# Batch 1's second scores a unit sooner, with k's evacuation on ScalarE, V copies on GpSimd, and W1 in 512-column pieces

## The chip, the cores and the metric

The kernel runs on one core of a Trainium2 chip. The metric is the device time in microseconds of one execution, as the median of several runs. A core has five engines that run side by side and meet at semaphores: TensorE (matrix products, and transposes by an identity), VectorE, ScalarE, GpSimd, and SyncE, which here only issues DMAs. Each engine takes its instructions in the order in which the program emits them, so an instruction that waits holds up all that follows it on its engine.

## The reference

```
# B, H, S, D = 8, 8, 576, 64
scores = q @ k^T / sqrt(D)                      # per batch and head
keep only 0 <= row - column < 64, softmax over columns
attn = softmax @ v                              # (B, H, S, D)
x  = attn with heads side by side               # (B, S, 512)
xn = (x - mean) / sqrt(var + 1e-6) * g_ln
out = x + relu(xn @ w_ch1) @ w_ch2              # 512 -> 2048 -> 512
```

Inputs and output are float32; the kernel computes its products in float16 with float32 sums.

## The kernel before, in words

The rows are cut into nine groups: group g (0 to 7) is the first 512 rows of batch g, group 8 the last 64 rows of all batches. A group has four blocks of 128 rows. Per block the attention is: **scores** (`s_pe`, L314, 32 small matmuls into PSUM), **exponentials** (`s_exp`, L350, ScalarE, two instructions), **mask** (`s_mask`, L362, VectorE, multiplies the probabilities by a 0/1 mask), **value step** (`b_pe`, L375, TensorE), and **rows** (`b_rows`, L397, VectorE: division by the row sums, mean and variance, and for groups 0 and 1 the z of the layer norm). `zt_step` (L461) transposes z; in groups 0 and 1 it does so on TensorE, with an evacuation from PSUM. The value step needs V in two layouts, `vA` (the block's rows) and `vB` (shifted by 64 rows): `vB_cur` and `vB_prev` (L181, L184) make the shifted one by copies across partitions. `t_main` (L259) transposes q (x=0) or k (x=1) of one half of a batch: eight transposes into PSUM and one evacuation by `evac` (L253), to ScalarE (0) or VectorE (1), x itself unless told otherwise.

The MLP of group g runs while the attention of batch g+1 is computed in between. `mlp_units` returns a list of units of TensorE work; after unit i, the steps that were put into slot i by `at(i, ...)` are emitted. So the order is written out by hand. Groups 0 and 1 start with half units (`l1_half`, L631: two 128-column chunks of W1 for 256 rows, eight matmuls of 256 columns). In group 0, two of them are replaced by `l1_rows` (L644), which works on one block of 128 rows at a time. The unit list of group 0 has 30 entries: eight of these, `l1` (L494) for the rest of W1, ten of `l2_three` (L672: the second layer for three blocks at once), and four parts of `l2` (L506) for the last block; `add_out` (L516, VectorE) then adds the product to x and frees its PSUM bank. Group 1 has 16 half units first. Their PSUM banks come from a pool of two (`ps_mm`), shared with the output banks of the second layer; each is free again when ScalarE has evacuated it with the relu (L641), or when `add_out` has read it.

W1 is loaded in eight pieces of 512 KB (`w1_load`, L195) on SyncE's queue, and scaled by g_ln into float16 by GpSimd or ScalarE (`w1_cast`, L213). The first four pieces hold all four 128-row chunks for 256 columns, the other four hold two chunks for 512 columns. W2 follows in eight pieces on the same queue (`w2_load`, `w2_cast`), with batch 1's q, k and V among them (`queue_up`, L940). `keep_clock(n)` (L882) emits n filler matmuls. `after_mask` (L359) is a one-column copy on GpSimd that reads the last masked probabilities, so that GpSimd's later instructions start after that mask. `part_vB` makes vB of later batches by DMA from vA.

Of the kernel before, what the change touches and what calls it, by code (L numbers as in the profile page):

```python
# [10 lines left out]
FP32 = mybir.dt.float32  # L11
# [7 lines left out]
def kernel(  # L19
# [166 lines left out]

    def part_vB(b, c, w=2):
        vB[b] = vB[b - 2]
        nc.sync.dma_start(out=vB[b][64:128, c:c + w], in_=vA[b][0:64, c:c + w])
        c0 = max(c, 1)  # L190
        nc.sync.dma_start(out=vB[b][0:64, c0:c + w], in_=vA[b][64:128, c0 - 1:c + w - 1])
# [3 lines left out]
    def w1_load(i):  # L195
        q2, pr = divmod(i, 2)
        if i < 4:
            t = p_wst.tile([128, NKC, HID // 8], FP32, tag="wld", name=f"w1s_{i}")[:, :, :]
            wst[("w1", i)] = t
            nc.sync.dma_start(  # L200
                out=t, in_=moe_w_ch1[:, (HID // 8) * i:(HID // 8) * (i + 1)].rearrange("(c p) n -> p c n", p=128),
            )
            return
        t = w2s[:, 4 * (i - 4):4 * (i - 3), :].rearrange("p c n -> p (c n)").bitcast(FP32).rearrange(
            "p (c n) -> p c n", c=2)
# [7 lines left out]
    def w1_cast(i, k0=0, k1=NKC, act=False):  # L213
        q2, pr = divmod(i, 2)
        t = wst[("w1", i)]
        if i < 4:
            for kc in range(k0, k1):
                o, sc = w1g[:, kc, (HID // 8) * i:(HID // 8) * (i + 1)], gT[:, kc:kc + 1]
                if act:
                    nc.scalar.activation(out=o, in_=t[:, kc], func=AF.Identity, bias=0.0, scale=sc)  # L220
                else:
                    nc.gpsimd.tensor_scalar(out=o, in0=t[:, kc], scalar1=sc, scalar2=1.0, op0=ALU.mult, op1=ALU.mult)
            return
        dst = w1g[:, 2 * pr:2 * pr + 2, (HID // 4) * q2:(HID // 4) * (q2 + 1)]
        for c in range(2):
            kc = 2 * pr + c
            nc.gpsimd.tensor_scalar(out=dst[:, c], in0=t[:, c], scalar1=gT[:, kc:kc + 1], scalar2=1.0,
                                    op0=ALU.mult, op1=ALU.mult)
# [256 lines left out]
    def mlp_units(g, split=0, three=False, seven=True):  # L485
# [158 lines left out]
        def l1_rows(kb):  # L644
            for i in range(2):
                if kb == 2:
                    pool, tag = ((ps_mm, "mm"), (ps_s, "sc"))[i]
                    rows_ps[i] = pool.tile([128, 2, 256], FP32, tag=tag, name=f"hph_{g}_1_{i}")
                c0 = 128 * (kb - 2)
                for e in range(2):  # L650
                    hc = 2 * i + e
                    for kc in range(NKC):
                        nc.tensor.matmul(
                            out=rows_ps[i][:, e, c0:c0 + 128], lhsT=w1g[:, kc, 128 * hc:128 * (hc + 1)],
                            rhs=zT[g][:, kc, 128 * kb:128 * kb + 128], start=(kc == 0), stop=(kc == NKC - 1),
                        )
                if kb == 3:
                    nc.scalar.activation(out=hrT[:, 2 * i:2 * i + 2, 256:512], in_=rows_ps[i],
                                         func=AF.Relu, bias=0.0, scale=1.0)

        rows_ps = {}

# [131 lines left out]
        if g == 0:  # L794
            halves = [(0, 0), (0, 1), (0, 2), 2, 3, (0, 3), (1, 2), (1, 3)]
        for u in halves:
            if isinstance(u, int):
                units.append(lambda u=u: l1_rows(u))
            else:
                units.append(lambda half=u[0], i=u[1]: l1_half(half, i))  # L800
# [120 lines left out]
    w1_cast(0, 0, 2)  # L921
    w1_cast(1, 0, 3)
    for i in range(2, 8):
        w1_cast(i)
# [10 lines left out]
    w1_cast(0, 2, 4, True)  # L935
    s_mm(0, 3, True)
    w1_cast(1, 3, 4, True)
    z_step(0, 2)

    def queue_up():  # L940
# [16 lines left out]
        cast_v(1, 2, 3)  # L957
        cast_v(1, 3, 4)
        load_qk(2, 0)
# [9 lines left out]
    for g in range(NGRP):  # L969
# [19 lines left out]
        if g == 0:  # L989
            at(0, b_step, 0, 3)  # L990
            at(0, queue_up)
            at(1, zt_step, 0, 2)
# [229 lines left out]
```

## Time and profile before

| | us |
|---|---|
| median of 3 runs | 304.95 (304.7 to 305.51) |
| the profiled execution's own time | 304.41 |
| its span, first to last instruction | 302.7 |
| TensorE busy | 292.3 (97%) |
| VectorE, ScalarE, GpSimd busy | 207.7, 156.2, 158.5 |
| mean granted TensorE clock | 0.996 |

The profile is one execution. In its timeline a row has the start, the busy time, the engine, the program line, the operation with the tiles written and read, the count, and in brackets the idle time of the engine ahead of it with what ended it. The span is shorter than the execution's time by 1.71 us, which lies around it.

### The profile page before, as it was taken

Reading aid. Unit: us, or ns where it says so; the run is one execution under the profiler, and the core shown is the slowest. Engines: PE = TensorE matmul, PEld = TensorE weight load, DVE = VectorE, ACT = ScalarE, POOL = GpSimd, SP = SyncE. Lnnn points to the kernel's source line nnn. Section 1 sums busy time; section 2 is a strip of 40 time slices with the busy share of each in tenths; the row PEclk is TensorE's granted clock in tenths of the full one; section 3 lists DMA queues with packets and bytes.
Section 4 is the critical chain, followed back from the end, with each engine's and each line's share of the span. In section 5 each row is a group of like instructions: output and inputs, shape, how many; then the busy total and the mean of one; then the engine's idle time right before and its main releaser. Section 6 shows DMA issues by size and latency. Waiting matters only on the chain.

```text
span 302.7 us, 7604 instructions
## 1 busy us (share of the span) xinstructions
PE 292.3 (97%) x3081; PEld 195.4 (65%) x3081; DVE 207.7 (69%) x408; ACT 156.2 (52%) x265; POOL 158.5 (52%) x238
## 2 busy tenths in 40 slices
PE   8999999989999999999999999999999999999992
PEld 3557545777454478547854786469646854788881
DVE  1881328684847886579766866698567775879972
ACT  3585645768358633874177428851664056216400
POOL 4689974543641886188608860897048307115200
PEclk9999999999999999999999999999999999999998
DMA  8999999999787999999299997992729396013014
GB/s 187 259 358 341 384 284 289 255 313 246 146 207 227 209 216 144 284 266 165 49 285 281 202 160 231 318 165 38 220 63 164 69 223 152 11 41 117 1 37 104
DMA packets 115044, 58.34 MB, mean 193 GB/s; under 512 B 83649, under 2 KB 106753, under 8 KB 115010
## 3 DMA queue, kind: packets, MB, share of 16 engines
q1 hardware_dynamic: 114720, 57.47, 79.7%
q8 instruction: 24, 0.39, 0.6%
q10 hardware_dynamic: 290, 0.40, 0.5%
q14 instruction: 10, 0.08, 0.1%
HBM read 38.80 MB, written 9.44 MB: 159 GB/s over the span
## 4 chain that ended last, share of the span: by engine, by line
PE 81%; DMA 7%; SPq 4%; ACT 3%; POOL 1%; issue 0%; DVE 0%
PE hps L494 28%; PE pA L571 12%; PE pB L571 8%; PE pC L571 8%; PE ch L506 5%; PE hph L636 5%; PE xps L394 3%; PE sc L347 3%; DMA w1s<-in_moe_w_ch_dram 3%; DMA wT<-in_moe_w_ch_dram 3%; PE lA L710 2%; DMA w2s<-in_moe_w_ch_dram 2%; SPq L167 2%; PE tp L274 2%; SPq L87 1%; PE lC L710 1%
## 5 line engine op out<-in xcount | busy, mean ns | idle before, releaser
L494 PE MATMUL hps<-zT,w1g 128*128 128x512 f16 x416 | 94.8, 379 | 0.0
L498 ACT ACTIVATE hrT<-hps 128x512 f16<-128x512 f32 x104 | 62.4, 600 | 41.2 <-PE hps L494 37.8
L494 PEld LDWEIGHTS <-w1g 128*128 128x128 f16 x416 | 39.2, 98 | 45.5 <-issue 2.2
L357 ACT ACTIVATE pt<-sc 128x512 f16<-128x512 f32 x72 | 39.5, 602 | 19.6 <-PE sc L347 18.8
L571 PEld LDWEIGHTS <-sS 128*128 128x128 f16 x448 | 43.3, 98 | 4.9
L446 POOL TENSOR_SCALAR rsz<-mvg 128x1 f32<-128x1 f32 x28 | 9.7, 346 | 69.3 <-DVE mvg L419 67.3
L367 DVE TENSOR_TENSOR pt<-pt,mask 128x1024 f16<-128x1024 f16 x32 | 23.4, 735 | 22.4 <-ACT pt L357 22.4
L145 POOL CAST qk<-qk 128x1024 f16<-128x1024 f32 x30 | 33.4, 1129 | 9.4 <-DMA qk<-in_q_dram 3.5
L571 PEld LDWEIGHTS <-hrT 128*128 128x128 f16 x336 | 32.1, 98 | 6.4 <-ACT hrT L498 1.0
L255 ACT COPY qkT<-tp 128x1024 f16<-128x1024 f16 (+1 forms) x17 | 16.4, 963 | 24.9 <-PE tp L274 22.9
L571 PE MATMUL pC<-w2s,sS 128*128 128x256 f16 x224 | 26.9, 273 | 0.0
L571 PE MATMUL pA<-wT,sS 128*128 128x256 f16 x224 | 26.9, 273 | 0.0
L414 DVE TENSOR_TENSOR xn<-xps,rcp 128x256 f32<-128x256 f32 (+1 forms) x50 | 25.8, 539 | 0.8
L416 DVE BATCH_NORM_STATS2 stats<-xn 128x6 f32<-128x512 f32 x36 | 25.0, 695 | 1.2
L545 DVE TENSOR_TENSOR sS<-hrT 128x512 f16<-128x512 f16 (+1 forms) x40 | 24.2, 605 | 2.1 <-ACT hrT L498 2.0
L636 PE MATMUL hph<-zT,w1g 128*128 128x256 f16 x176 | 22.3, 273 | 1.3 <-ACT hrT L641 0.4
L452 POOL TENSOR_SCALAR z<-xn,rsz 128x512 f16<-128x512 f32 x24 | 21.5, 895 | 2.5
L410 DVE RECIPROCAL rcp<-xps 128x4 f32<-128x4 f32 (+1 forms) x50 | 8.0, 181 | 19.0 <-PE xps L394 18.9
L447 POOL TENSOR_TENSOR rsz<-rsz,mhalf 128x1 f32<-128x1 f32 x28 | 18.5, 661 | 2.3
L636 PEld LDWEIGHTS <-w1g 128*128 128x128 f16 x176 | 16.4, 98 | 4.6 <-issue 1.3
L506 PE MATMUL ch<-w2s,hrT 128*128 128x512 f16 x80 | 18.8, 379 | 0.0
L173 POOL CAST vA<-v 128x1024 f16<-128x1024 f32 (+1 forms) x18 | 15.4, 873 | 4.9 <-DMA v<-in_v_dram 4.6
(121 smaller groups left out, 429.3 us busy)
## 6 DMA issues: line engine op xcount, KB each, us to landing
out_dram<-xn SPq DMA_DIRECT2D x33, 256.0 KB, 3.0
qk<-in_q_dram SPq DMA_DIRECT2D x16, 512.0 KB, 6.2
qk<-in_k_dram SPq DMA_DIRECT2D x16, 512.0 KB, 7.0
v<-in_v_dram SPq DMA_DIRECT2D x28, 256.0 KB, 6.9
w2s<-in_moe_w_ch_dram SPq DMA_DIRECT2D x9, 512.0 KB, 8.1
w1s<-in_moe_w_ch_dram SPq DMA_DIRECT2D x4, 512.0 KB, 7.4
tk<-in_k_dram SPq DMA_DIRECT2D x8, 256.0 KB, 4.7
tv<-in_v_dram SPq DMA_DIRECT2D x8, 256.0 KB, 5.2
```

Of the source, the lines that this page charges most:

```text
L145: nc.gpsimd.tensor_copy(out=dst[:, :].rearrange("p (a j) e d -> p a e j d", j=j), in_=t[:, :].rearrange("p (a e j d) -> p a e j d", e=2, j ...
L357: nc.scalar.activation(out=o, in_=i, func=AF.Exp, bias=0.0, scale=scale)
L367: nc.vector.tensor_tensor(out=ptv, in0=ptv, in1=mb, op=ALU.mult)
L414: nc.vector.tensor_tensor(out=xn[:, n * i:n * i + n], in0=xps[:, :, 0:D], in1=rcp_b, op=ALU.mult)
L416: nc.vector.bn_stats(out=stats, in_=xv)
L452: nc.gpsimd.tensor_scalar(out=z, in0=xv, scalar1=rs, scalar2=nm, op0=ALU.mult, op1=ALU.add)
L494: nc.tensor.matmul(out=hps, lhsT=w1g[:, kc, 128 * hc:128 * (hc + 1)], rhs=zT[g][:, kc, :], start=(kc == 0), stop=(kc == NKC - 1),)
L498: nc.scalar.activation(out=hrT[:, hc, :], in_=hps, func=AF.Relu, bias=0.0, scale=1.0)
L506: nc.tensor.matmul(out=ch[kb], lhsT=hrT[:, hc, 128 * kb:128 * (kb + 1)], rhs=w2s[:, hc, :], start=(hc == 0), stop=(hc == NHC - 1),)
L545: nc.vector.tensor_tensor(out=o, in0=x, in1=y, op=op)
L571: nc.tensor.matmul(out=o, lhsT=a[:, c, 128 * p:128 * p + 128], rhs=wv[:, c, :], start=(first and (p == 0 or split_c) and c == 0), stop=(c ...
L636: nc.tensor.matmul(out=hps[:, e], lhsT=w1g[:, kc, 128 * hc:128 * (hc + 1)], rhs=zT[g][:, kc, 256 * half:256 * half + 256], start=(kc == 0) ...
```

## The change

W1's first four pieces take the form of the other four: two 128-row chunks by 512 columns. `w1_cast` gets a list of chunks; GpSimd casts all but two chunks, the second ones of pieces 1 and 3, which ScalarE casts. Group 0's units become eight plain half units; `l1_rows` goes. Batch 0's last value step (`b_step(0, 3)`) moves from behind the first unit to ahead of it, behind two filler matmuls. The evacuation of z's block 2 moves from ScalarE to VectorE.

For batch 1's second half: k's evacuation moves from VectorE to ScalarE; the three shifted V copies move from ScalarE, in slots 27 and 28, to GpSimd, in `queue_up`; the scores of blocks 2 and 3 move from slot 29 to 28, ahead of group 0's last unit; block 3's exponentials come with them, and its mask moves from group 1 into slot 29. In group 1, the value steps move from slot 3 to 1, the z transposes from 6 and 7 to 4 and 6, and batch 2's transposes from 4, 5, 6, 7 to 2, 3, 5, 7. On GpSimd `after_mask` comes after one cast of batch 2 instead of three, and V's casts move from slot 5 to 0.

```diff
+    def shift_v(p, c):
+        nc.gpsimd.tensor_copy(out=vB[1][p:p + 64, c + (p == 0), :, 0:D], in_=vq(1, c, c + 1)[64 - p:128 - p, 0])
...
     def w1_load(i):
         q2, pr = divmod(i, 2)
         if i < 4:
-            t = p_wst.tile([128, NKC, HID // 8], FP32, tag="wld", name=f"w1s_{i}")[:, :, :]
...
+            t = p_wst.tile([128, 2, HID // 4], FP32, tag="wld", name=f"w1s_{i}")[:, :]
+        else:
...
-    def w1_cast(i, k0=0, k1=NKC, act=False):
+    def w1_cast(i, cs=(0, 1), act=False):
...
+        for c in cs:
             kc = 2 * pr + c
+            o, sc = w1g[:, kc, (HID // 4) * q2:(HID // 4) * (q2 + 1)], gT[:, kc:kc + 1]
+            if act:
+                nc.scalar.activation(out=o, in_=t[:, c], func=AF.Identity, bias=0.0, scale=sc)
+            else:
+                nc.gpsimd.tensor_scalar(out=o, in0=t[:, c], scalar1=sc, scalar2=1.0, op0=ALU.mult, op1=ALU.mult)
...
-        if g == 0:
-            halves = [(0, 0), (0, 1), (0, 2), 2, 3, (0, 3), (1, 2), (1, 3)]
...
-    w1_cast(0, 0, 2)
-    w1_cast(1, 0, 3)
-    for i in range(2, 8):
-        w1_cast(i)
+    for i in range(8):
+        w1_cast(i, (0,) if i in (1, 3) else (0, 1))
...
-    w1_cast(0, 2, 4, True)
     s_mm(0, 3, True)
-    w1_cast(1, 3, 4, True)
+    w1_cast(1, (1,), True)
     z_step(0, 2)
+    keep_clock(2)
+    b_step(0, 3)
...
         cast_qk(1, 1)
         cast_v(1, 2, 3)
+        shift_v(64, 2)
+        shift_v(0, 2)
         cast_v(1, 3, 4)
+        shift_v(64, 3)
...
         if g == 0:
-            at(0, b_step, 0, 3)
+            at(0, w1_cast, 3, (1,), True)
             at(0, queue_up)
-            at(1, zt_step, 0, 2)
+            at(1, zt_step, 0, 2, "dve")
...
-            at(26, t_main, 1, 1, 1, 1)
+            at(26, t_main, 1, 1, 1, 0)
             at(26, lambda: tbank.update(n=0))
             at(27, zt_step, 1, 1)
-            at(27, vB_cur, 1, 2, 0)
-            at(28, vB_prev, 1, 2, 0)
-            at(28, vB_cur, 1, 3, 0)
-            at(29, s_pe, 1, 2)
-            at(29, s_pe, 1, 3, False, "t")
-            at(29, s_exp, 1, 2, 0, 1)
-            at(29, s_mask, 1, 2)
+            at(28, s_pe, 1, 2)
+            at(28, s_pe, 1, 3, False, "t")
+            at(28, s_exp, 1, 2, 0, 1)
+            at(28, s_mask, 1, 2)
+            at(28, s_exp, 1, 3, 0, 1)
+            at(29, s_mask, 1, 3)
         if g == 1:
-            at(0, s_exp, 1, 3, 0, 1)
-            at(0, s_mask, 1, 3)
-            at(0, cast_qk, 2, 0)
-            at(0, cast_qk, 2, 1, (0,))
+            at(0, cast_qk, 2, 0, (0,))
             at(0, after_mask, 1, 3)
-            at(0, cast_qk, 2, 1, (1,))
-            at(3, b_pe, 1, 2, "t")
-            at(3, b_pe, 1, 3, "sc")
-            at(3, b_rows, 1, 2)
-            at(4, b_rows, 1, 3)
-            at(6, zt_step, 1, 2)
-            at(4, root, 1)
-            at(7, zt_step, 1, 3)
-            at(4, alloc_v, 2)
-            at(4, alloc_qkT, 2)
+            at(0, cast_qk, 2, 0, (1,))
+            at(0, cast_qk, 2, 1)
+            at(0, alloc_v, 2)
+            at(0, alloc_qkT, 2)
             for c in (0, 2):
-                at(5, cast_v, 2, c, c + 2)
+                at(0, cast_v, 2, c, c + 2)
                 at(5, part_vB, 2, c)
-            at(4, t_main, 2, 0, 0)
-            at(5, t_main, 2, 1, 0)
-            at(6, t_main, 2, 0, 1)
+            at(1, b_pe, 1, 2, "t")
+            at(1, b_pe, 1, 3, "sc")
+            at(1, b_rows, 1, 2)
+            at(2, b_rows, 1, 3)
+            at(2, root, 1)
+            at(2, t_main, 2, 0, 0)
+            at(3, t_main, 2, 1, 0)
+            at(4, zt_step, 1, 2)
+            at(5, t_main, 2, 0, 1)
+            at(6, zt_step, 1, 3)
             at(7, t_main, 2, 1, 1)
```

More of the change, by code (lines that the diff above doesn't have):

```diff
@@ L197, in w1_load @@
         if i < 4:
-            t = p_wst.tile([128, NKC, HID // 8], FP32, tag="wld", name=f"w1s_{i}")[:, :, :]
[L199 to L205, printed above, removed]
+            t = p_wst.tile([128, 2, HID // 4], FP32, tag="wld", name=f"w1s_{i}")[:, :]
+        else:
+            t = w2s[:, 4 * (i - 4):4 * (i - 3), :].rearrange("p c n -> p (c n)").bitcast(FP32).rearrange(
+                "p (c n) -> p c n", c=2)
         wst[("w1", i)] = t
@@ L211, in w1_load @@
         )
-    def w1_cast(i, k0=0, k1=NKC, act=False):
+    def w1_cast(i, cs=(0, 1), act=False):
         q2, pr = divmod(i, 2)
         t = wst[("w1", i)]
[L216 to L225, printed above, removed]
-            kc = 2 * pr + c
-            nc.gpsimd.tensor_scalar(out=dst[:, c], in0=t[:, c], scalar1=gT[:, kc:kc + 1], scalar2=1.0,
-                                    op0=ALU.mult, op1=ALU.mult)
+        for c in cs:
+            kc = 2 * pr + c
+            o, sc = w1g[:, kc, (HID // 4) * q2:(HID // 4) * (q2 + 1)], gT[:, kc:kc + 1]
[3 more added lines that the diff above has]
+                nc.gpsimd.tensor_scalar(out=o, in0=t[:, c], scalar1=sc, scalar2=1.0, op0=ALU.mult, op1=ALU.mult)
     def w2_load(i):
@@ L642, in l1_half @@
                                  func=AF.Relu, bias=0.0, scale=1.0)
[L644 to L661, printed above, removed]
         def l2_three(i):
@@ L793, in mlp_units @@
         halves = [(half, i) for half in range(2) for i in range(split // 2)]
-        if g == 0:
-            halves = [(0, 0), (0, 1), (0, 2), 2, 3, (0, 3), (1, 2), (1, 3)]
[L796 to L800, printed above, removed]
+        for half, i in halves:
+            units.append(lambda half=half, i=i: l1_half(half, i))
         for hc in range(split, NHC):
```

## The prediction

> **What bounds the kernel now.** I read the page's chain first, then TensorE's own waits, then its timeline.
>
> ```profile
> PE 81%; DMA 7%; SPq 4%; ACT 3%; POOL 1%; issue 0%; DVE 0%
> ```
>
> TensorE carries 81% of the chain that ended last, so an edit on another engine is worth what it takes off a TensorE wait. Of TensorE's waits, summed over the run (us in total, times, longest), four lie behind its start-up:
>
> ```profile
> PE tp L274 <- ACT qkT L255: 0.6, 2, 0.3
> PE ch L672 <- POOL w2s L241: 0.5, 1, 0.5
> PE hph L636 <- ACT hrT L641: 0.4, 1, 0.4
> PE hph L636 <- ACT zT L474: 0.4, 1, 0.4
> ```
>
> TensorE's timeline (start us, busy us) puts these four between 45 and 66 us; after 66 us its only gap is 0.03 us.
>
> ```profile
> 45.71 2.32 PE L672 MATMUL ch<-w2s,hrT 128*128 128x512 f16 x10 [0.48 <-POOL w2s L241]
> ...
> 53.76 3.00 PE L636 MATMUL hph<-zT,w1g 128*128 128x256 f16 x24
> 57.19 1.03 PE L636 MATMUL hph<-zT,w1g 128*128 128x256 f16 x8 [0.43 <-ACT hrT L641]
> ...
> 60.13 1.04 PE L636 MATMUL hph<-zT,w1g 128*128 128x256 f16 x8
> 61.44 0.61 PE L274 MATMUL tp<-ident,qk 128*128 128x128 f16 x8 [0.27 <-ACT qkT L255]
> ...
> 64.30 0.39 PE L471 MATMUL ztp<-ident,z 128*128 128x128 f16 x4
> 65.00 0.61 PE L274 MATMUL tp<-ident,qk 128*128 128x128 f16 x8 [0.31 <-ACT qkT L255]
> 65.97 1.91 PE L636 MATMUL hph<-zT,w1g 128*128 128x256 f16 x16 [0.37 <-ACT zT L474]
> ```
>
> The brackets understate the loss, because a row's busy time includes the pipe's drain; I take start to start. One half unit (8 matmuls of 256 columns) steps 63.42 to 64.30 = 0.88, eight transposes 62.98 to 63.42 = 0.44, four 62.75 to 62.98 = 0.23. So the three units from 53.76 should have ended at 56.40, not 57.19: 0.79 lost. 60.13 + 0.88 = 61.01, not 61.44: 0.43. 64.30 + 0.23 = 64.53, not 65.00: 0.47. 65.00 + 0.44 = 65.44, not 65.97: 0.53. Together 2.22 us in the stretch that the change rewrites. Before 45.71, the last value step starts at 45.04 and such a step passes to the next matmul in 0.13 (58.67 to 58.80), so 0.54 is lost there. All that can be won from 45 us on is 2.76 us.
>
> Why the first two happen is in ScalarE's timeline, where the V copies stand ahead of the scores' exponentials, and those around the evacuations of the first units:
>
> ```profile
> 52.18 1.90 ACT L255 CAST vB<-v 64x512 f16<-64x512 f32 x3
> 54.10 1.09 ACT L357 ACTIVATE pt<-sc 128x512 f16<-128x512 f32 x2
> 55.07 0.61 ACT L641 ACTIVATE hrT<-hph 128x512 f16<-128x512 f32 x1
> 55.54 1.11 ACT L357 ACTIVATE pt<-sc 128x512 f16<-128x512 f32 x2
> 56.50 1.14 ACT L641 ACTIVATE hrT<-hph 128x512 f16<-128x512 f32 x2
> ```
>
> **W1 in 512-column pieces.** The first four pieces had rows of 1 KB, the later ones and W2 have 2 KB. Two windows, the first in the 1 KB pieces, the second in W2 (the last columns are TensorE's clock, DMA share, GB/s):
>
> ```profile
> 18.00:20.00 2.00, 2.00 (x38) 1.18 (x32) 1.66 (x4) 1.81 (x4) 1.33 (x3) 1.00 1.09 348
> 34.00:38.00 4.00, 4.00 (x49) 1.87 (x48) 0.82 (x1) 2.84 (x6) 4.00 (x5) 1.00 1.04 386
> ```
>
> Four pieces are 2.10 MB: 6.03 us at 348 GB/s, 5.43 at 386, so 0.60 saved on one queue that is backed up from the first load until the last W2 piece, whose landing ends the 0.54 wait. TensorE must also get there no later. Now the first unit needs two pieces, and two filler matmuls and batch 0's last value step come ahead of it. That step still waits for exponentials that end at 20.19, and ends near 20.6 as now; the first unit, 19.00 now, starts there. Its third k-chunk (GpSimd, 0.68 a cast, near 20.0) and fourth (ScalarE after 20.19, about 0.7 as its 0.72 z from SBUF) are in time. So are the third unit's, near 22.9, if the pieces land 0.15 closer together than now. From 20.66, eight units (8 x 0.88) and two z transposes (2 x 0.23) end at 28.16, against 28.18 now: the casts' waits of now pay for the later start. The row-wise units fall away at no gain (32 matmuls of 128 columns in 1.79, 16 of 256 in 1.76). GpSimd makes 14 casts of 0.68 instead of 13 of 0.47 and 8 of 0.68, some 2 us less, and is ahead of W2's pieces either way. If the pieces don't speed up, the third unit waits 0.4, which the W2 wait absorbs. So this part is worth 0 to -0.54; I take -0.54, since the later pieces already show the rate.
>
> **Scores a unit sooner, V copies off ScalarE, k's evacuation onto it.** k's evacuation costs 1.0 on ScalarE (1.01 for q's) where it idles 0.93 ahead of 51.57, with z's 0.73 done at 50.63, so it ends near 51.6 and the scores' last operand is there in time. Three V copies go to GpSimd: 3 x 0.65 (0.61 to 0.69 there) between 49.5 and 52.5, where GpSimd otherwise idles between 51.1 and 52.87; what comes next, the batch 2 query cast, waits for its data until 52.74. The copies are needed by the value steps after 55 us, so they cost nothing; if that cover failed, 1.9 us is their price. The scores now start one output step (4 x 0.216 = 0.87) sooner, 52.32 instead of 53.19, with ScalarE free: four exponentials (0.48 apart) end at 54.4 to 54.8 instead of 56.65, so both bank waits of ScalarE (the 0.79) go.
>
> What comes late instead is on VectorE:
>
> ```profile
> 38.07 0.69 DVE L367 TENSOR_TENSOR pt<-pt,mask 128x1024 f16<-128x1024 f16 x1 [3.25 <-ACT pt L357]
> 39.05 1.15 DVE L367 TENSOR_TENSOR pt<-pt,mask 128x1024 f16<-128x1024 f16 x1 [0.29 <-ACT pt L357]
> ...
> 53.30 0.75 DVE L516 SCALAR_TENSOR_TENSOR xn<-ch,rstdg,xn 128x512 f32<-128x512 f32 x1 [1.07 <-PE ch L506]
> ```
>
> Group 0's last output add (L516, 53.30 now) frees the PSUM bank that group 1's second unit writes. It now stands behind the mask of block 2, which waits for two exponentials. In the earlier instance scores at 36.51 gave a mask at 38.07, 1.56 later. So: 52.32 + 1.56 = 53.88, + 0.69 = 54.57, + 0.75 = 55.32, and the second unit, due at 53.76 + 0.88 = 54.64, starts at about 55.34: a new wait of 0.70. Its ends: 0 if the mask started at once, 1.19 if the mask takes the 1.18 it shows at 55.22 while GpSimd casts (the 1.15 above is the same). GpSimd's one cast there ends at 53.91, so I take 0.69.
>
> The Trainium skill, GPSIMD Engine Reference (section Key points), says that GpSimd shares its SBUF interfaces with VectorE and collides with instructions in a 2-port mode or with two SBUF inputs, which speaks against moving copies there. The mask rows agree (0.69 alone, 1.15 beside casts); by the rule alone the mask would be priced at 1.18 and the total below would be 0.49 smaller; I don't, because the copies end before the mask begins.
>
> **Value steps behind unit 1, batch 2's transposes one a unit.** The value steps then run near 56.3 (second mask: 55.3 + 0.69 = 56.0). Their rows (2.4 us of VectorE each) finish z near 59.1 and 61.4, wanted after units 4 and 6 at about 60.8 and 63.0. ScalarE's evacuations (1.01) now have two units between the transposes that share a bank, and unit 7 stands between the last z evacuation and unit 8: the 0.47 and the 0.53 go. The k transposes still follow q's by one unit and wait for q's evacuation: the 0.43 stays. GpSimd is held until the second mask (after_mask, about 56.0), and behind it wait batch 2's k cast and the later q, k and V: k is ready near 57.1, wanted at 59.2. SP's V shifts for batch 2 go out when V's casts are done, near 62 instead of 65.5 to 68, and are wanted at 71. All have 2 us or more.
>
> **Sum.** -0.54 (W2) - 0.79 - 0.47 - 0.53 + 0.70 = -1.63. Nothing waits later, so the shift reaches the end. The profiled execution took 304.41 (302.7 span and 1.71 around it): 302.8. The median of the runs is 304.95, 0.54 above it: 303.3.
>
> **The rivals.** What this measurement can tell from no change is 0.3%, 0.92 us here.
> 1. The W2 piece lands no sooner: an HBM limit rather than row length, or GpSimd late. Against it stand the two windows. -1.09 alone: 303.9.
> 2. VectorE becomes the wait: GpSimd's casts fall on the mask, which takes 1.18, so the second unit waits 1.19, and W2 gains nothing: -1.09 + 0.49 = -0.60, 304.4, no change that can be told. For it: both masks were stretched so in this stretch. Against: here only one cast stands near, and it ends first.
> 3. Slower: the clock. Between the fillers (end 19.45) and the value step (20.1) TensorE idles 0.65, then the first unit may wait. In the first 6.6 us the filler matmuls stepped 0.43 and then half that, so TensorE has a half rate that lasts about 5.5 us. If it falls back at 20, half of that, 2.75 us, is lost; 0.54 falls into the W2 wait, which then gains nothing: -1.09 + 2.75 - 0.54 = +1.12, 306.1. The sign turns once the loss passes 1.63 us. Against: TensorE idled 0.52 at 17.12 with the clock at 1.00.
>
> The Trainium skill, TensorE: Matmul & The Clock Gate (Part 1), lets the clock fall only after an idle window of about 3.4 us; by it this rival is nil, and no run here shows such an idle window.
>
> **How the numbers follow.** Forecast 0.52 (302.6 to 304.0), rival 1 0.20, rival 2 0.17, rival 3 0.11. Faster takes the forecast and most of rival 1 (which lies 0.1 inside the bound), 0.67; same the rest of it and rival 2, 0.21; slower 0.12. The low end adds k's 0.43 and a nearly absent new wait: 304.95 - 2.5 = 302.4; the high end takes in rival 2: 304.8.
>
> **What would show it.** Right: no wait of L672 on w2s; ScalarE's exponentials before 55 us in one run of four; L516's last add behind a mask, and one wait of L636 of 0.5 to 0.7 on it near 55; one wait left of L274 on qkT; group 1's ninth unit about 1.6 us before 65.97. Wrong: a TensorE wait on GpSimd in group 1, a clock below 1.00 between 19 and 28 us, or new waits past 66 us.

## The result, and the profile after

| | before | after |
|---|---|---|
| median of 5 runs, us | 304.89 (304.39 to 305.51) | 303.51 (302.68 to 303.91) |
| ratio of the times | | 0.9953, 95% interval 0.9932 to 0.9974 |
| profiled execution, us | 304.41 | 303.51 |
| its span, us | 302.7 | 301.2 |
| mean granted TensorE clock | 0.996 | 0.997 |

The change made the kernel faster by 1.4 us; 303.3 was forecast. The profiled pair differs by 0.90 us only, since the profiled execution of the kernel before lies 0.48 below that kernel's median. The chain that ended last still runs on TensorE:

```profile
PE 81%; DMA 8%; SPq 5%; POOL 2%; ACT 1%; DVE 1%; issue 0%; POOLq 0%
```

The line numbers have moved: the half units are L629 now, their relu L634, W2's first use L646, the output add L509, the mask L360, the exponentials L350, the transposes of q and k L267, the evacuations L248. TensorE's own waits after the change (us in total, times, longest):

```profile
PE hph L629 <- DVE xn L509: 0.5, 1, 0.5
...
PE tp L267 <- POOL qk L145: 0.3, 1, 0.3
PE tp L267 <- ACT qkT L248: 0.3, 1, 0.3
PE ch L646 <- POOL w2s L234: 0.2, 1, 0.2
PE hph L629 <- POOL w1g L221: 0.2, 1, 0.2
```

Of the four waits of before, that on the relu and that on z's evacuation are gone, that on q's evacuation stays once instead of twice, and that on W2 has halved. New are the wait on the add, which was forecast, and a wait of the transposes on GpSimd's cast of q, which was not. TensorE's timeline puts them in place:

```profile
45.29 2.32 PE L646 MATMUL ch<-w2s,hrT 128*128 128x512 f16 x10 [0.24 <-POOL w2s L234]
47.91 0.62 PE L267 MATMUL tp<-ident,qk 128*128 128x128 f16 x8 [0.30 <-POOL qk L145]
...
53.82 1.04 PE L629 MATMUL hph<-zT,w1g 128*128 128x256 f16 x8
55.35 1.03 PE L629 MATMUL hph<-zT,w1g 128*128 128x256 f16 x8 [0.49 <-DVE xn L509]
...
59.59 0.61 PE L267 MATMUL tp<-ident,qk 128*128 128x128 f16 x8 [0.27 <-ACT qkT L248]
...
64.87 1.36 PE L629 MATMUL hph<-zT,w1g 128*128 128x256 f16 x11
```

W2's first use starts 0.42 us sooner than before (45.29 against 45.71), but the first unit of group 1 starts no sooner (53.82 against 53.76): the wait at 47.91 took it all back. From the first unit to the ninth it is 11.05 us instead of 12.21. So in this pair of executions the whole gain lies in the rewritten stretch, and what W1 won is lost again before it. On ScalarE and VectorE that stretch looks much as forecast:

```profile
52.82 2.06 ACT L350 ACTIVATE pt<-sc 128x512 f16<-128x512 f32 x4 [0.61 <-PE sc L340]
```

```profile
53.93 0.71 DVE L360 TENSOR_TENSOR pt<-pt,mask 128x1024 f16<-128x1024 f16 x1 [3.02 <-ACT pt L350]
54.56 0.74 DVE L509 SCALAR_TENSOR_TENSOR xn<-ch,rstdg,xn 128x512 f32<-128x512 f32 x1
55.22 0.68 DVE L360 TENSOR_TENSOR pt<-pt,mask 128x1024 f16<-128x1024 f16 x1
```

The four exponentials stand in one run, the mask of block 2 starts at 53.93 (forecast 53.88), the add behind it at 54.56 (54.57), and the second unit at 55.35 (55.34).

### The profile page after: what moved, and what is told of

Same layout as the page of the kernel before. It is cut to its first block, busy times and chain, and to the rows that moved or that the text cites. A ratio compares the mean times of both kernels' runs of the same rounds, so it can differ in the third digit from the quotient of the medians.

```text
span 301.2 us, 7568 instructions
## 1 busy us (share of the span) xinstructions
PE 291.7 (97%) x3067; PEld 195.3 (65%) x3067; DVE 208.1 (69%) x408; ACT 155.1 (51%) x261; POOL 159.2 (53%) x234
## 4 chain that ended last, share of the span: by engine, by line
PE 81%; DMA 8%; SPq 5%; POOL 2%; ACT 1%; DVE 1%; issue 0%; POOLq 0%
PE hps L487 28%; PE pA L564 12%; PE pB L564 8%; PE pC L564 8%; PE ch L499 6%; PE hph L629 4%; DMA w2s<-in_moe_w_ch_dram 3%; PE xps L387 3%; DMA wT<-in_moe_w_ch_dram 3%; PE sc L340 3%; PE lA L684 2%; PE tp L267 2%; DMA qk<-in_q_dram 2%; SPq L167 2%; SPq L206 2%; SPq L87 1%
## 5 line engine op out<-in xcount | busy, mean ns | idle before, releaser
L487 PEld LDWEIGHTS <-w1g 128*128 128x128 f16 x416 | 39.3, 98 | 45.4 <-issue 2.2
L350 ACT ACTIVATE pt<-sc 128x512 f16<-128x512 f32 x72 | 39.3, 600 | 21.5 <-PE sc L340 20.8
L360 DVE TENSOR_TENSOR pt<-pt,mask 128x1024 f16<-128x1024 f16 x32 | 23.5, 737 | 22.5 <-ACT pt L350 22.5
L248 ACT COPY qkT<-tp 128x1024 f16<-128x1024 f16 (+1 forms) x18 | 17.4, 964 | 24.7 <-PE tp L267 23.1
L629 PE MATMUL hph<-zT,w1g 128*128 128x256 f16 x192 | 23.5, 273 | 0.7 <-DVE xn L509 0.5
L629 PEld LDWEIGHTS <-w1g 128*128 128x128 f16 x192 | 18.0, 98 | 3.5 <-issue 0.7
```

The costliest lines, as they stand in the source:

```text
L350: nc.scalar.activation(out=o, in_=i, func=AF.Exp, bias=0.0, scale=scale)
L360: nc.vector.tensor_tensor(out=ptv, in0=ptv, in1=mb, op=ALU.mult)
L487: nc.tensor.matmul(out=hps, lhsT=w1g[:, kc, 128 * hc:128 * (hc + 1)], rhs=zT[g][:, kc, :], start=(kc == 0), stop=(kc == NKC - 1),)
L629: nc.tensor.matmul(out=hps[:, e], lhsT=w1g[:, kc, 128 * hc:128 * (hc + 1)], rhs=zT[g][:, kc, 256 * half:256 * half + 256], start=(kc == 0) ...
```

## One table for all runs

Every execution can be cut at three points of TensorE's timeline: the start of group 1's first unit, the start of its ninth, and the start of the last matmul. "End" is what follows the last matmul's start, up to the execution's time. All numbers are us of the profiled execution; the four columns add up to its time. The last column is the ratio of the times to those of the kernel before, from the runs that were timed beside it, with its 95% interval. The kernel before was timed anew beside each group of runs (medians from 304.68 to 305.23), so times of different groups are compared by these ratios.

| kernel | to 1st unit | 1st to 9th | 9th to last matmul | end | time | ratio |
|---|---|---|---|---|---|---|
| before | 53.76 | 12.21 | 230.44 | 8.00 | 304.41 | 1 |
| after | 53.82 | 11.05 | 230.39 | 8.25 | 303.51 | 0.9953 [0.9932, 0.9974] |
| e1, W1 alone | 53.56 | 12.21 | 230.38 | 7.77 | 303.92 | 0.9965 [0.9953, 0.9977] |
| e2, all but W1 | 54.28 | 11.04 | 230.42 | 8.06 | 303.80 | 0.9960 [0.9946, 0.9973] |
| e3, add first | 53.37 | 10.53 | 230.39 | 8.21 | 302.50 | 0.9938 [0.9923, 0.9952] |
| e4, k a unit later | 53.42 | 10.77 | 230.43 | 8.23 | 302.85 | 0.9931 [0.9916, 0.9946] |
| e5, casts on masks | 53.61 | 11.14 | 230.38 | 8.20 | 303.33 | 0.9950 [0.9936, 0.9963] |
| e6, V on ScalarE | 53.41 | 12.59 | 230.39 | 7.89 | 304.28 | 0.9980 [0.9969, 0.9991] |
| e7, scores late | 53.78 | 11.00 | 230.39 | 8.18 | 303.35 | 0.9951 [0.9933, 0.9969] |
| e8, batch 1's q, k later | 53.68 | 10.79 | 230.39 | 8.28 | 303.14 | 0.9937 [0.9924, 0.9951] |
| e9 = e3 + e4 | 53.32 | 10.09 | 231.02 | 8.14 | 302.57 | 0.9931 [0.9910, 0.9951] |
| e10 = e9 + e8 + V shifts first | 53.76 | 10.10 | 230.93 | 8.16 | 302.95 | 0.9940 [0.9926, 0.9953] |
| e11, four fills more | 53.85 | 11.04 | 230.38 | 8.36 | 303.63 | 0.9961 [0.9947, 0.9975] |
| e12, e8 with the old W1 | 54.75 | 10.78 | 230.72 | 8.05 | 304.30 | 0.9981 [0.9972, 0.9990] |

The column "1st to 9th" is steady to 0.01 us where its order of work is the same (before and e1; after, e2 and e11). The column "to 1st unit" is not: it varies by 0.5 us between executions of kernels with the same work ahead of the first unit (53.32 to 53.85). So verdicts on the rewritten stretch can rest on single profiles, and verdicts on W1 can't.

## The experiments

### W1 alone, and all but W1

e1 is the changed kernel with slots 26 to 29 of group 0 and group 1's slots 0 to 7 as before; e2 is the kernel before with those slots, and the GpSimd copies, as changed.

```diff
# e1, against the changed kernel
-        shift_v(64, 2)
-        shift_v(0, 2)
...
-            at(28, s_pe, 1, 2)
+            at(29, s_pe, 1, 2)
...
-            at(1, b_pe, 1, 2, "t")
+            at(3, b_pe, 1, 2, "t")
```

> The kernel before with W1's pieces, the half units and batch 0's last value step as in the change, and nothing from slot 26 of group 0 on. Theory: the pieces bring W2's last piece some 0.4 us sooner, but batch 1's second q and k, behind it on the queue, land no sooner, and TensorE waits for q's cast near 47.9 us instead: 0 to -0.1 us in all, group 1's ninth unit at 65.9. Rival: that late landing was chance in one execution of the change, and the pieces are worth -0.4 to -0.5 us, the ninth unit at 65.5.

> The kernel before with everything from slot 26 of group 0 on as in the change (scores a unit sooner, k on ScalarE, V copies on GpSimd, value steps behind unit 1), W1 as before. Theory: it carries the whole change: -1.1 us, the ninth unit at 64.87, with the 0.5 us wait on W2 at 45.7 still there. Rival: -0.7 us or less, the rest being W1's.

e2 did what its theory said in the stretch: 11.04 us from first to ninth unit, and a time 0.40% lower (interval 0.27% to 0.54%), 1.2 us. Its ninth unit came at 65.32 instead of 64.87, because W2 was late. e1 left that stretch at 12.21, as expected, but gained 0.35% (interval 0.23% to 0.47%), 1.1 us, more than either expectation. Its own profile shows only a part of that: the last matmul starts 0.26 sooner, the end is 0.23 shorter. The rest is in which executions were profiled: e1's had a span of 302.1, near its median of 301.95, while before's had 302.7, and the median span of the 17 runs of before timed beside it was 303.2. What differs between executions is seen at W2's first use. In e2 and in e1:

```profile
46.22 2.32 PE L675 MATMUL ch<-w2s,hrT 128*128 128x512 f16 x10 [0.84 <-POOL w2s L244]
```

```profile
45.51 2.32 PE L646 MATMUL ch<-w2s,hrT 128*128 128x512 f16 x10 [0.48 <-POOL w2s L234]
```

e2 has the old W1 pieces like the kernel before, yet it waits 0.84 where before waited 0.48: W2's last piece landed at 45.08 there and at 44.57 before. One pair of profiles can't price W1. The times don't price it well either: the two parts, 0.35% and 0.40%, add up to more than the whole's 0.47%, and on top of e2 the new pieces bring 0.07%, which the intervals don't tell from nothing.

### The gate behind W2's: the cast of q

The wait at 47.91 was the second question. In the changed kernel q of batch 1's second half landed at 46.69 and was cast by 47.85; in the kernel before it landed at 46.34 and was cast by 47.51, 0.36 ahead of its transposes at 47.87. GpSimd's rows for that cast, before and after:

```profile
46.47 1.04 POOL L145 CAST qk<-qk 128x1024 f16<-128x1024 f32 x1 [0.81 <-DMA qk<-in_q_dram]
```

```profile
46.81 1.04 POOL L145 CAST qk<-qk 128x1024 f16<-128x1024 f32 x1 [1.57 <-DMA qk<-in_q_dram]
```

The forecast had not looked at this margin. e8 puts those transposes one output step later:

```diff
-            at(24, t_main, 1, 0, 1, 0)
+            at(25, t_main, 1, 0, 1, 0)
             at(25, zt_step, 1, 0)
             at(26, z_step, 1, 1)
-            at(26, t_main, 1, 1, 1, 0)
             at(26, lambda: tbank.update(n=0))
+            at(27, t_main, 1, 1, 1, 0)
             at(27, zt_step, 1, 1)
```

> The changed kernel with the transposes of batch 1's second q and k put one output step later, behind the z work of the same slot. Theory (behind the wait for W2's last piece there is a second gate, the cast of q that lands at 46.7 us, which gave a new idle time of 0.30 us at 47.91 and so took back what W2 had won): the wait on that cast disappears from TensorE's waits, the first unit of group 1 starts 0.2 to 0.4 us sooner than the changed kernel's 53.82, and the time falls by as much. Rival (what TensorE reaches there is set by when the transfers happen to land, and some later gate, the scores or the evacuation of k, takes the gain): the first unit stays within 0.1 of 53.4 to 53.8 and the time within 0.15 of the changed kernel.

```profile
47.87 0.61 PE L267 MATMUL tp<-ident,qk 128*128 128x128 f16 x8
48.32 0.39 PE L464 MATMUL ztp<-ident,z 128*128 128x128 f16 x4
...
51.98 0.89 PE L340 MATMUL sc<-qkT,qkT 64*128 64x64 f16 x32
...
53.68 1.04 PE L629 MATMUL hph<-zT,w1g 128*128 128x256 f16 x8
```

The wait on the cast is gone, but the scores now come right behind the last transposes and wait for two evacuations: their 32 matmuls take 0.89 instead of 0.64. By its own execution e8 wins nothing ahead of the first unit, and q landed at 45.89 there, so that it would not have waited anyway. The executions of all kernels together show what it waits for. Where the order ahead of the first unit is that of before or after (before, e2, after, e1, e3 to e7, e9, e11), the first unit starts at the later of two times: 9.20 us behind the landing of W2's last piece, or 7.13 behind q's.

| kernel | W2's last piece lands | + 9.20 | q lands | + 7.13 | 1st unit |
|---|---|---|---|---|---|
| before | 44.57 | 53.77 | 46.34 | 53.47 | 53.76 |
| e2 | 45.08 | 54.28 | 46.83 | 53.96 | 54.28 |
| e9 | 44.11 | 53.31 | 45.81 | 52.94 | 53.32 |
| e7 | 44.58 | 53.78 | 46.38 | 53.51 | 53.78 |
| after | 44.14 | 53.34 | 46.69 | 53.82 | 53.82 |
| e5 | 44.07 | 53.27 | 46.47 | 53.60 | 53.61 |
| e11 | 44.30 | 53.50 | 46.72 | 53.85 | 53.85 |

The two constants were read off these executions, so the table is a fit; that two numbers meet these seven executions, and e1, e3, e4 and e6 too, to 0.01 is what speaks for it. With e8's edit the first unit comes 9.54 behind W2's landing (e8 44.14 and 53.68, e10 44.22 and 53.76, e12 45.21 and 54.75): in these three the edit pays 0.34 and no longer asks for q. It gains 0.26 from first to ninth unit, because the scores start hardly later while the first unit does, so the add's wait shrinks. By the profiles its net is about nothing. The rival had the first unit right (53.68, within its 53.4 to 53.8). The time fell by more than the 0.15 that it allowed, 0.9937 against 0.9953 or 0.5 us, but the intervals overlap, so whether the edit gains is not decided. Its spread was narrower: 303.01 to 303.30 in six runs of e8, 302.68 to 303.91 in five of the changed kernel.

### W1's price without the gate

> The run with the old W1 pieces and all else of the change, and in it the transposes of batch 1's second q and k an output step later: beside the same edit with the new W1 pieces (303.12) only W1 differs, and the cast of q no longer stands behind the wait for W2. Theory (W1 in 512-column pieces is worth the 0.4 to 0.55 us that the W2 wait shrinks by, once nothing behind it takes it back): 303.5 to 303.7, unit 0 of group 1 0.4 to 0.6 later than the 53.68 there. Rival (nothing is left of it, since the scores then wait for k's evacuation and z): time within 0.2 of 303.12.

```profile
46.35 2.32 PE L675 MATMUL ch<-w2s,hrT 128*128 128x512 f16 x10 [1.00 <-POOL w2s L244]
```

Between e12 and e8 only W1 differs. By the ratios it is 0.44% of the time, 1.3 us; by the profiles the first unit is 1.07 later, all of it from W2's landing (45.21 against 44.14), and another 0.33 is lost in a wait on an output add at 205 us that no other profile shows. Both expectations were too small. Over all profiles W2's last piece landed at 44.57, 45.08 and 45.21 with the old pieces (mean 44.95) and between 44.07 and 44.58 in eleven executions with the new ones (mean 44.23). So the new pieces bring W2 0.7 us sooner, with a scatter of up to 0.4 to either side, and only three of the fourteen profiles have the old pieces. The landing of q follows by 1.7 to 1.8 us in nine of the fourteen, and by 2.0 to 2.6 in five, all with the new pieces. Why it does so in some executions alone isn't settled.

### The add behind the mask

In the changed kernel block 2's mask stands ahead of the add on VectorE, which gave the wait that was forecast at 0.70 and came out at 0.65. e3 turns the two round:

```diff
             at(28, s_exp, 1, 2, 0, 1)
-            at(28, s_mask, 1, 2)
             at(28, s_exp, 1, 3, 0, 1)
+            at(29, s_mask, 1, 2)
             at(29, s_mask, 1, 3)
```

> The changed kernel with block 2's mask moved from slot 28 to 29, behind group 0's last output add on VectorE. Theory: the second unit's 0.66 us wait is the add standing behind the mask; the add then ends at 54.7 instead of 55.3, the masks end where they do now, and TensorE is 0.6 us earlier: -0.6 against the changed kernel, -1.7 against the one before. Rival: the value steps then wait for the masks instead, and nothing is won.

VectorE's rows in e3:

```profile
53.57 0.75 DVE L509 SCALAR_TENSOR_TENSOR xn<-ch,rstdg,xn 128x512 f32<-128x512 f32 x1 [2.40 <-PE ch L499]
54.24 1.28 DVE L360 TENSOR_TENSOR pt<-pt,mask 128x1024 f16<-128x1024 f16 x2
```

First to ninth unit 10.53 instead of 11.05: 0.52 of the 0.65 is had by turning two instructions round. The add's wait shrinks to 0.13, both masks run behind it (54.24 to 55.52), and the value steps aren't late.

### The scores a unit sooner

> The changed kernel with the scores, their exponentials and both masks of batch 1's blocks 2 and 3 put back by one output step, behind the last output add; V copies, k's evacuation and value steps stay as changed. Theory (the scores a unit sooner are worth nothing as long as the add stands behind their mask): the wait of the second unit on the add goes, exponentials and masks are 0.9 later and the bank waits on ScalarE are small because the copies are off it; first to ninth unit 10.6 to 11.0, time 0.1 to 0.4 below the changed kernel. Rival (the sooner scores carry the gain): value steps and the evacuations behind them come late, first to ninth unit 11.5 or more, time 0.5 above the changed kernel or worse.

e7 puts scores, exponentials and masks back by one output step: `at(28, ...)` becomes `at(29, ...)` in those five lines.

```profile
56.49 0.22 PE L387 MATMUL xps<-vB,pt 128*64 128x65 f16 x1 [0.41 <-DVE pt L360]
```

First to ninth unit 11.00 against 11.05, and the same time by the ratios (0.9951 against 0.9953). The wait on the add is gone, but the second value step waits for its mask (0.41). So the scores a unit sooner are worth nothing as long as the add stands behind the mask: one wait takes the place of the other. With the mask behind the add, as in e3, they are worth 0.5 (10.53 against 11.00).

### V copies back on ScalarE

```diff
-        shift_v(64, 2)
-        shift_v(0, 2)
...
-        shift_v(64, 3)
...
             at(27, zt_step, 1, 1)
+            at(27, vB_cur, 1, 2, 0)
+            at(27, vB_prev, 1, 2, 0)
+            at(27, vB_cur, 1, 3, 0)
```

> The changed kernel with the three V copies back on ScalarE, ahead of the exponentials, and none on GpSimd. Theory (the copies stand in ScalarE's queue ahead of the scores' exponentials, and everything behind follows: exponentials 1.3 us later, the mask, then the output add that stands behind it, then the second unit): the second unit waits about 1.8 us instead of 0.5, first to ninth unit about 12.3 instead of 11.05, time about 1.2 above the changed kernel, that is 304.7, no better than the kernel before. Rival (ScalarE has slack here, the gain came from the order of the steps alone): first to ninth unit at most 0.5 us longer, time within 0.5 of the changed kernel.

ScalarE's timeline, then TensorE's:

```profile
52.05 1.89 ACT L248 CAST vB<-v 64x512 f16<-64x512 f32 x3
53.96 2.06 ACT L350 ACTIVATE pt<-sc 128x512 f16<-128x512 f32 x4
```

```profile
56.49 0.70 PE L629 MATMUL hph<-zT,w1g 128*128 128x256 f16 x5 [2.04 <-DVE xn L509]
```

The copies stand ahead of the exponentials, the mask behind those, the add behind the mask, and the second unit behind the add: 2.04 of idle time. First to ninth unit 12.59, longer than before. Moving the V copies is what the sooner scores stand on: without it the stretch loses 1.54. By the ratios the whole change is then 0.20% faster than before instead of 0.47%; that it is faster at all fits the first unit (53.41) and the end (7.89), which both came out short in the profile.

### GpSimd's casts on the masks

```diff
-            at(0, cast_qk, 2, 0, (0,))
+            at(0, cast_qk, 2, 0)
+            at(0, cast_qk, 2, 1, (0,))
             at(0, after_mask, 1, 3)
-            at(0, cast_qk, 2, 0, (1,))
-            at(0, cast_qk, 2, 1)
+            at(0, cast_qk, 2, 1, (1,))
```

> The changed kernel with GpSimd's casts of batch 2's q and k queued ahead of the copy that holds them until the mask of block 3 is done, so that they run beside both masks. Theory (the second rival's mechanism, a mask with two SBUF inputs is stretched by GpSimd's casts): the masks take 1.15 to 1.25 us instead of 0.71 and 0.68, the add ends 0.5 later, the second unit's wait is about 1.0 instead of 0.5, time 0.4 to 0.6 above the changed kernel, near 304.0. Rival (the casts wait for their loads, which land from 52.3 on, and meet the masks only in part, or the masks do not mind): masks 0.7 to 0.9, time within 0.2 of the changed kernel.

GpSimd's casts, then VectorE's masks:

```profile
54.35 1.07 POOL L145 CAST qk<-qk 128x1024 f16<-128x1024 f32 x1 [0.37 <-DMA qk<-in_k_dram]
55.80 1.06 POOL L145 CAST qk<-qk 128x1024 f16<-128x1024 f32 x1 [0.38 <-DMA qk<-in_q_dram]
```

```profile
53.72 0.80 DVE L360 TENSOR_TENSOR pt<-pt,mask 128x1024 f16<-128x1024 f16 x1 [2.69 <-ACT pt L350]
...
55.10 0.86 DVE L360 TENSOR_TENSOR pt<-pt,mask 128x1024 f16<-128x1024 f16 x1
```

The rival was right: the casts wait for their loads and meet each mask only in part. The masks take 0.80 and 0.86 instead of 0.71 and 0.68, first to ninth unit is 0.09 longer, and the time is the same.

What a cast costs a mask can be read more exactly, since it repeats. In the kernel before, VectorE's and GpSimd's rows are:

```profile
55.22 1.18 DVE L367 TENSOR_TENSOR pt<-pt,mask 128x1024 f16<-128x1024 f16 x1 [1.17 <-ACT pt L357]
```

```profile
54.82 1.04 POOL L145 CAST qk<-qk 128x1024 f16<-128x1024 f32 x1 [0.91 <-PE hph L636]
```

Where a cast is already running when the mask starts, the mask takes its 0.69 and, on top, what is left of the cast less 0.15:

| kernel | cast ends | mask starts | left of the cast | mask took | over 0.69 |
|---|---|---|---|---|---|
| before | 55.86 | 55.22 | 0.64 | 1.18 | 0.49 |
| before | 57.39 | 56.69 | 0.70 | 1.24 | 0.55 |
| after | 54.10 | 53.93 | 0.17 | 0.71 | 0.02 |
| after | 69.29 | 68.42 | 0.87 | 1.42 | 0.73 |
| e5 | 53.97 | 53.72 | 0.25 | 0.80 | 0.11 |
| e5 | 55.42 | 55.10 | 0.32 | 0.86 | 0.17 |
| e4 | 53.84 | 53.53 | 0.31 | 0.85 | 0.16 |

Where the mask starts first it is the cast that is longer. e1 has the GpSimd order of the kernel before; there VectorE's and GpSimd's rows are:

```profile
56.48 0.69 DVE L360 TENSOR_TENSOR pt<-pt,mask 128x1024 f16<-128x1024 f16 x1 [0.78 <-ACT pt L350]
```

```profile
56.62 1.45 POOL L145 CAST qk<-qk 128x1024 f16<-128x1024 f32 x1 [2.03 <-PE hph L629]
```

0.55 of the mask was left at 56.62, and the cast took 1.45 instead of 1.04. Both hold throughout: in the fourteen profiles, all 44 masks that start while such a cast of q or k runs, and all 34 such casts that start while a mask runs, fit within 0.01 us (the cast's 1.04 and what is left of the mask less 0.14; with less than that left, nothing is added). So the two don't share; the later one stands until the earlier is nearly done. The Trainium skill says so: SBUF — State Buffer (SBUF: two separate sides; Who interferes with whom) has the port pair of VectorE and GpSimd as an exclusive lock that whoever starts first holds for the whole instruction, and a VectorE instruction with two SBUF inputs as one that contends with GpSimd's reads. These rows agree, up to the 0.15. The forecast priced the mask at either 0.69 or 1.18; by this reading it is 0.69 plus what is left of a running cast less 0.15, here 0.02.

### The k transposes, and all edits together

```diff
# e4
             at(2, t_main, 2, 0, 0)
-            at(3, t_main, 2, 1, 0)
             at(4, zt_step, 1, 2)
+            at(4, t_main, 2, 1, 0)
```

> The changed kernel with batch 2's first k transposes moved from slot 3 to 4, behind z's. Theory: the 0.43 us wait of the k transposes for ScalarE's evacuation of q is only the one unit between them: with two units it is gone, -0.43 against the changed kernel, -1.5 against the one before. Rival: k's evacuation on VectorE or z's comes later in turn and a wait of like size appears ahead of the ninth unit or the next scores.

> The changed kernel with two edits of earlier runs together: block 2's mask is queued behind group 0's last output add, and batch 2's second k transpose goes in a unit later, behind the z transposes. Theory (the add that stands behind the mask and the k transpose that waits for q's evacuation are two separate waits of TensorE, so they add up): the first edit took unit 0 to unit 8 from 11.05 to 10.53 us, the second to 10.77, so together 11.05 - 0.52 - 0.28 = 10.25, or 10.1 if the add's wait, which had grown by 0.15 in the second, is gone too; time 0.8 to 0.95 below the changed kernel's 303.51, about 302.6. Rival (one slack is shared, the later wait grows when the earlier one goes): unit 0 to unit 8 stays at 10.5 or above, time about 303.0.

The two waits are separate: e4 takes 0.28 (the 0.43 of k, with a wait on the add that grew by 0.15), e3 0.52, and both together 0.96, 11.05 to 10.09. But 0.6 of it comes back at 71 us, in a wait that the runs before it did not have:

```profile
71.00 0.19 PE L387 MATMUL xps<-vB,pt 128*64 128x65 f16 x1 [0.56 <-DMA vB<-vA]
```

Batch 2's V shift, issued at 63.22 behind the loads of batch 3's q and k, had landed 2.1 us ahead of its use in the kernel before (70.81 and 72.94) and 0.5 ahead in the changed one (71.36 and 71.83). A unit stream that runs ahead meets it. e10 issues the first half ahead of those loads and takes e8's edit in:

```diff
-                at(5, part_vB, 2, c)
+                at((3, 5)[c // 2], part_vB, 2, c)
```

> The changed kernel with the add ahead of the mask, the second k transpose a unit later, the transposes of batch 1's second q and k an output step later, and one edit more: the first half of batch 2's V shifts is issued ahead of the load of batch 3's q and k instead of behind it. Theory (in the run with the first two edits the new 0.56 us wait of the value steps at 71.0 was the V shift, issued at 63.22 behind those loads and landed at about 71; issued ahead of them, at about 62, it lands about 1.2 us sooner): no wait on vB, first to ninth unit 10.1 or less, last matmul 0.6 to 0.9 us sooner than that run's 294.43, time about 302.0, 1.5 below the changed kernel. Rival (the transfers' own latency of 7 us decides, not their place): a wait of 0.3 to 1.0 on vB stays or moves to the load of batch 3's q, time 302.6 or more.

```profile
89.95 1.25 PE L487 MATMUL hps<-zT,w1g 128*128 128x512 f16 x5 [0.41 <-DMA zT<-z]
```

The V shift's wait is gone: its first transfer, issued at 61.12, landed at 65.51, after 4.4 us, where e9's took 7.65 (63.22 to 70.87). So its place behind the loads made it late, as the theory had it, and not a latency of its own; it came 5.4 us sooner, more than the 1.2 expected. First to ninth unit is 10.10, but the next gate is a DMA transpose of z at 90 us (0.57 start to start), and e8's edit costs its 0.34. So the expected 302.0 was missed: 302.95. In e10 SyncE issues the transposes of z some 2.2 us later than in e9 (the last of that group at 87.48 instead of 85.32); what ahead of them on its queue made them late was not tested. e9, e4, e8, e3 and e10 lie within one another's intervals, at 0.9931 to 0.9940 of before; by the ratios each beats the changed kernel by 0.4 to 0.7 us, but every one of these intervals overlaps that of the changed kernel. Of the 0.96 us that e9 takes out of the rewritten stretch, 0.6 is handed to the next wait; the best times lie near 302.8 to 303.1, whichever of these edits are in.

### The end of the kernel

> The changed kernel with four one-element fills more on GpSimd, late in group 1, where GpSimd idles: 238 instructions there as in the kernel before, instead of 234. Nothing waits for them. Theory (the kernel's end has a fixed part that goes with the number of GpSimd's instructions: 5.97 us from the last matmul to the end of the span with 231 or 234 of them, 6.3 with 238 or 241; and 2.2 from the span to the time with 234, 1.75 with 238 and 241): last matmul to span's end 6.3, time minus span 1.7 to 1.8, the sum 0.1 to 0.2 below the changed kernel's. Rival (these parts hang on the code's place or on another engine): 5.97 and 2.2 as in the changed kernel.

The span went on for 6.28 us behind the start of the last matmul before and 5.97 after, and the time was 1.72 longer than the span before and 2.28 after. With e11's four fills these are 6.42 and 1.94, together 8.36. So the first part goes with GpSimd's instructions, as the theory had it: 5.95 to 5.98 in all kernels with 231 or 234 of them, 6.28 to 6.42 with 238 or 241. It is a step and not a slope, and four instructions more also move the code behind them, so whether the count or the code's place decides is not shown. The second does not follow that count alone (1.82 to 1.92 with 231, 2.18 to 2.30 with 234, 1.72 to 1.94 with 238 and 241), and the sum did not fall. Its cause stays open. For the change, the profiles show 0.25 us lost at the end, which no wait of TensorE shows.

## Why the prediction was right, step by step

**Right in sum.** The forecast's sum was -1.63, all of it on TensorE. By the medians the kernel gained 1.38. Of the sum's two halves one is shown, term by term; that the other was met is in part luck.

**The rewritten stretch, -1.09: measured -1.16.** The bank waits (0.79), the wait on k's bank (0.47) and that on z's evacuation (0.53) went, the k transposes kept theirs (0.43), and the new wait came out at 0.65 instead of 0.70. The terms close: 12.21 - 2.22 + 0.65 + 0.43 is 11.07, and 11.05 was measured. e2 shows it without W1 (11.04), and e6 shows that nothing of it is left without the V copies' move (12.59). e7 shows that the sooner scores by themselves brought nothing (11.00 without them), close to the forecast's -0.79 + 0.70. No run puts the value steps and batch 2's transposes back alone; that the 0.47 and 0.53 are theirs is read from TensorE's rows. The masks took 0.71 and 0.68: the cast that stood near ended 0.17 into the first, so that the copies and casts on GpSimd cost 0.02, as the lower price had it. The cast was to end at 53.91, by the mask's start; it ended at 54.10, because the V copies ran until 52.99 and put its start off to 53.06. The price of 1.18 would have needed a cast that starts 0.4 us ahead of the mask.

**W1, -0.54: the transfers came sooner as priced; what that is worth is not settled.** The pieces land 1.35 us apart instead of 1.50 (17.86 to 21.91 against 18.02 to 22.52), so the fourth lands 0.64 sooner, on the mean over the eleven executions with the new pieces and the three with the old, where 0.60 was priced. SyncE begins to issue the last W2 piece 0.51 sooner (37.19 against 37.70), and it lands 0.72 sooner; the 0.2 beyond the priced rate is not explained. By the table's two gates the first unit comes at 54.15 on the mean of the three executions with the old pieces and at 53.56 on that of the eleven with the new ones, without e8's edit: -0.59. In the profiled pair the cast of q took all of it back. The times give 0.35% (e1), 0.07% (the change beside e2) and 0.44% (e12 beside e8), which is 0.2 to 1.3 us. Two steps of the working failed here. The first was that "TensorE must also get there no later" was the only condition: behind the W2 wait came a transfer with 0.36 to spare. The second was the claim of a queue backed up until the last W2 piece. The windows from 41 on, in the kernel before and then in the changed one (last two columns DMA share, GB/s), show thin spots ahead of its landing:

```profile
41.00:42.00 1.00, 1.00 (x6) 0.47 (x5) 0.00 (x0) 0.00 (x0) 0.63 (x2) 1.00 0.64 107
```

```profile
18.00:20.00 2.00, 1.59 (x32) 0.68 (x32) 1.75 (x5) 1.31 (x3) 1.93 (x3) 1.00 1.05 371
...
40.00:41.00 1.00, 1.00 (x6) 0.42 (x5) 0.02 (x1) 0.00 (x0) 1.00 (x2) 1.00 0.89 156
...
43.00:44.00 1.00, 1.00 (x6) 0.44 (x5) 0.00 (x0) 0.98 (x2) 0.47 (x1) 1.00 0.68 206
```

The first row of the second fence is the one that was priced: 371 GB/s now where it was 348, on the way to the 386 that was assumed. That part held; the rate at the end of W2 is another.

**Early on.** The first unit was to start at 20.66 and started at 20.18; one wait of 0.20 on a W1 cast at 22.74 is left, and the 512-column units begin at 28.00 against 28.18. No clock below 1.00 shows in the windows from 18 to 30 us. The third rival's condition did not arise: its idle time of 0.65 came out as 0.27, so what a longer one would do is not shown.

**What was not seen.** "All have 2 us or more" was wrong for the V shifts: 0.5 is left. It cost this change nothing and e9 0.6. And the sum stopped at the last matmul; the end behind it grew by 0.25.

**The signs named ahead.** Right: the run of four exponentials, the add behind a mask, one wait of 0.5 to 0.7 on it, one wait left on q's evacuation, no new wait past 66 us, the clock. Wrong: W2's wait was to vanish (0.24 is left), and the ninth unit was to come 1.6 sooner (1.10 in the profile).

## What to carry to other kernels

When a wait on a transfer is to shrink, list the transfers that land behind it with their margins at their uses: unless these land sooner too, the gain is no larger than the smallest margin, here 0.36 us in the kernel before. Two gates can be checked over many executions as the later of two landing times plus a constant. An instruction that ends a wait of TensorE should not be queued behind one that waits for another engine: turning the mask and the add round took 0.52 us out of TensorE's stretch by moving one line. And where a stretch runs ahead by a microsecond, look at the DMAs that it uses: the V shift, queued behind two loads, became the next wait, and with a place ahead of them it landed 5.4 us sooner.

## What the runs showed of the hardware

- With the same work ahead of it, W2's last piece landed between 44.07 and 44.58 us in eleven executions, one of each kernel, while TensorE's own stretch from first to ninth unit repeats to 0.01 us where its order is the same. How much of the scatter of the times (302.7 to 303.9 in five runs of the changed kernel) comes from such landings is not shown, since one execution of each kernel has a trace.
- Four loads of 512 KB landed 1.50 us apart with rows of 1 KB (18.02 to 22.52) and 1.35 apart with rows of 2 KB (17.86 to 21.91).
- A shift of V between partitions by DMA took 4.4 us from issue to landing ahead of two 512 KB loads (e10) and 7.65 behind them (e9).
- VectorE's mask and GpSimd's casts exclude each other: the one that starts second stands until the first is nearly done (in the rows shown, 0.02 to 0.73 us added to a mask, 0.41 to a cast).
- The end of the program is not constant: 7.77 to 8.36 us from the start of the last matmul to the execution's time, in kernels that differ by up to ten GpSimd instructions; what sets it stays open.
